# Attention and a gated MLP in one kernel: the key maxima go through DRAM, and the work around block 2's first pair of weight chunks is re-placed

## The chip, the cores and the metric

One core of a Trainium2 chip runs the kernel. The metric is the device time of one execution in microseconds (us). A core has TensorE (PE: matmuls, with their weight loads as PEld), VectorE (DVE), ScalarE (ACT), GpSimd (POOL) and SyncE (SP). In this kernel nearly every transfer between DRAM and the core's memory is issued by SP, one after the other, in the order of SP's list.

## The reference

Two softmaxes (of q over its features, of k over the sequence), two small matrix products for each head, and then a two-layer MLP over the 4608 tokens with the gate h * clip(h + 3, 0, 6) / 6:

```python
q_s = np.exp(q - np.max(q, axis=-1, keepdims=True))
q_s = q_s / (np.sum(q_s, axis=-1, keepdims=True) + 1e-09)
k_s = np.exp(k - np.max(k, axis=2, keepdims=True))          # max over the 576 positions
k_s = k_s / (np.sum(k_s, axis=2, keepdims=True) + 1e-09)
kv = np.einsum('bhsd,bhse->bhde', k_s, v)
x = np.einsum('bhsd,bhde->bhse', q_s, kv)                   # (8, 8, 576, 64), then 4608 x 512
h = x @ w_in                                                # 4608 x 2048
g = h * np.clip(h + 3.0, 0.0, 6.0) / 6.0
return g @ w_out                                            # 4608 x 512
```

q, k and v are float32, the weights are float64. Every float32 operand of a large product is split into a high and a low part, and three products (high by high, high by low, low by high) stand for one.

## The kernel before

The 4608 tokens are 9 blocks j of 512, the 2048 hidden features are 16 chunks f of 128. Blocks 0 and 1 go chunk by chunk (`gemm1`, then `gemm2`). From block 2 on (`FAST = 2`) two chunks make a pair, and `fast_pair` computes the pair's first product with 7 half-size products (Strassen's scheme in Winograd's form) instead of 8; each is 6 matmuls of 256 columns. `product(n, ...)` writes one of three PSUM tiles: z (shown as `pz`), x and y (both `ph`, two buffers). The x tile is written four times in a pair and must be emptied in between: by ACT's copies (lines 544, 555, 563), and at the end by `swish(r[:, HT:], x)`, an ACT operation (line 534) and then a DVE one (line 535). The next pair's product 1 writes the same buffer.

Between the products, `fill(n)` issues n matmuls of the second product (`po`, 512 columns) for the chunks that are pending. A usual pair has 7 x 6 half-size matmuls and 24 `po` matmuls. After each stretch `tick(j, n)` runs the steps that a table sets for that place: block j + 1's attention is spread over block j's 64 ticks, 8 to a pair. `half(j, a, b, begin)` holds the table for two of the four head pairs; its first numbers are ticks relative to `begin`. The steps that matter here: `load_k` (the transposed keys `kt`, one buffer), `k_max` (the maximum of each key feature over the sequence, `km`, one number to a partition), `k_turn` (a TensorE transpose of `km`, spread over 128 columns, against the identity: afterwards every partition holds all 128 maxima, in PSUM as `pm`), `k_sub` and `k_exp` (the keys `ke` less these maxima, then the exponential), and the q steps (`q_stat`, `q_swap`, `q_sub`, `q_exp`, `q_over`, `q_mul`, `q_turn`). `pm` takes a buffer of the pool `ps_a` (two buffers), from which `pz`, `pkv` and `px` come as well.

The weights' sums for a pair (`fast_weights`) are made in block 1 for pairs 0 to 6 and stored to DRAM. For pair 7 they are made in block 2, in six pieces that `next(pieces)` runs at ticks. Their intermediate sums s12 and s34 take the two `ob` buffers, which also hold block 1's results until their store to DRAM has landed.

What sets the order: PE keeps the program's order from block 1 on; DVE, ACT and POOL keep it from block 2 on. SP's list is laid out by the framework's scheduler, and SP waits at each transfer for what that transfer needs (data, a free buffer), with all later ones queued behind it. The ring of weights that SP fetches (`w<-wf`) holds 12 products, so that a fetch is issued when its place comes free and is needed 12 products later.

Of the kernel before, what the change touches and what calls it, by code (L numbers as in the profile page):

```python
# [10 lines left out]
F32 = mybir.dt.float32  # L11
# [3 lines left out]
ALU = mybir.AluOpType  # L15
# [3 lines left out]
P = 128  # L19
TB = 512  # L20
# [10 lines left out]
def attention_moe(  # L31
# [27 lines left out]
    nc = tc.nc  # L59

    B, NP, _, S = kT.shape
    D = q.shape[5]
    NT, DM = out.shape
    NB = NT // TB
    NFC = w.shape[0]
    NCC = DM // P
    NTT = TB // P
    NCH = S // P + 1
# [5 lines left out]
    att = ctx.enter_context(tc.tile_pool(name="att", bufs=1))  # L74
    xp = ctx.enter_context(tc.tile_pool(name="xp", bufs=2))
    moe = ctx.enter_context(tc.tile_pool(name="moe", bufs=2))
    dr = ctx.enter_context(tc.tile_pool(name="dr", bufs=1, space=bass.MemoryType.DRAM))
    ps_a = ctx.enter_context(tc.tile_pool(name="ps_a", bufs=2, space=PSUM))
# [6 lines left out]
    def ordered(ins):  # L85
        if in_order:
            tc.keep_in_program_order(ins)
# [8 lines left out]
    def flip(out, in_):  # L96
        ordered(nc.tensor.transpose(out, in_, ident))  # L97
# [23 lines left out]
    def split(hi, lo, src, engine=nc.vector):  # L121

        nc.scalar.copy(hi, src)  # L123
        engine.tensor_sub(lo, src, hi.bitcast(F32))  # L124

    def load_w(f, sides=(0, 1)):
        if f not in raws:
            raws[f] = place(f, U32, f"raw{f}")
        a, b = 2 * DM * sides[0], 2 * DM * (sides[-1] + 1)
        nc.sync.dma_start(  # L130
            raws[f][:, a:b], w[f].rearrange("p s n -> p (s n)")[:, a:b]
        )
# [39 lines left out]
    FAST = 2  # L172
# [235 lines left out]
    X11, X21, X22, T1, T2, T3, T4 = range(7)  # L408
# [46 lines left out]
    def fast_weights(pair):  # L455

        a, b = wi[2 * pair], wi[2 * pair + 1]
        kept[pair] = d = dr.tile([P, 7, 2, HT], F32, name=f"wf{pair}")
        for n, src in ((A11, a[:, :, 0:HT]), (A12, a[:, :, HT:]), (A22, b[:, :, HT:])):
            nc.sync.dma_start(d[:, n], src.bitcast(F32))  # L460
        whole = moe.tile([P, 2 * DM], F32, name="m", tag="v", bufs=3)
        for at, src in ((0, a), (TB, b)):
            nc.vector.tensor_add(
                whole[:, at : at + TB], src[:, 0].bitcast(F32), src[:, 1].bitcast(F32)
            )
            yield
        a11, a12, a21, a22 = (whole[:, n * HT : (n + 1) * HT] for n in range(4))
        hi, lo = (t.rearrange("p e n -> p (e n)") for t in (a, b))
        s12, s34 = (moe.tile([P, DM], F32, name="ob", bufs=2) for _ in range(2))
        s1, s2, s3, s4 = (t[:, n : n + HT] for t in (s12, s34) for n in (0, HT))  # L470
        nc.vector.tensor_add(s1, a21, a22)
        nc.vector.tensor_sub(s2, s1, a11)
        yield
        split(hi[:, 0:TB], lo[:, 0:TB], s12)
        yield
        nc.vector.tensor_sub(s3, a11, a21)
        nc.vector.tensor_sub(s4, a12, s2)
        yield
        split(hi[:, TB:], lo[:, TB:], s34)
        for e, t in enumerate((hi, lo)):  # L480
            nc.sync.dma_start(
                d[:, S1 : S4 + 1, e], t.bitcast(F32).rearrange("p (k n) -> p k n", k=4)
            )
# [10 lines left out]
    def fetch(count):  # L494
        for _ in range(count):
            key = next(wanted, None)
            if key is None:
                return
            j, pair, n = key
            f, h = RING[next(turn) % len(RING)]  # L500
            t = wi[f].rearrange("p a n -> p (a n)")[:, h * TB : (h + 1) * TB]
            t = t.rearrange("p (e n) -> p e n", e=2)
            nc.sync.dma_start(t.bitcast(F32), kept[pair][:, ORDER[n][0]])
            come[key] = t
# [80 lines left out]
    plan = {}  # L585
# [4 lines left out]

    def half(j, a, b, begin):

        kts, kes, vts, qts, kms, qms, swaps, qTs = ({} for _ in range(8))
        has_k = j < B
        i = a % 2
        to = factors(j)
# [6 lines left out]
        has = {}  # L603
# [17 lines left out]
                kms[hp] = att.tile([P, 1], F32, name="km", bufs=2)  # L621
                nc.vector.tensor_reduce(kms[hp], kts[hp], axis=AX.X, op=ALU.max)  # L622

        def k_turn(hp):
            if has_k:
                has["pm"] = ps_a.tile([P, TB], F32, name="pm", tag="pa")
                flip(has["pm"][:, 0:P], kms[hp].broadcast_to([P, P]))

        def k_sub(hp):
            if has_k:  # L630
                ke, pm = kes[hp], has["pm"][:, 0:P].rearrange("p (o n) -> p o n", o=1)
                nc.vector.tensor_sub(ke, ke, pm.broadcast_to([P, NCH, P]))

        def k_exp(hp):
            if has_k:
# [101 lines left out]
        def part(n, src):  # L737
            return lambda: split(to[n][:, 0, i], to[n][:, 1, i], src())

        def ts(n):  # L740
            return has["ts"][:, n * HT : (n + 1) * HT]
# [27 lines left out]
        def on(fn, *args):  # L769
            return lambda: fn(*args)  # L770
# [2 lines left out]
            (-12, on(load_k, a)),  # L773
            (-11, on(load, a)),
            (-8, on(load, b)),
            (0, on(k_max, a)),
            (1, on(load_k, b)),
            (1, on(q_stat, a, ALU.max)),
            (2, on(k_turn, a)),
            (2, on(q_swap, a)),  # L780
            (3, on(k_sub, a)),
            (4, on(k_exp, a)),
            (4, on(q_sub, a)),
            (5, on(q_exp, a)),
            (5, on(k_max, b)),
            (6, on(q_stat, a, ALU.add)),
            (7, on(q_swap, a)),
            (7, on(q_stat, b, ALU.max)),
            (8, on(q_over, a)),
            (8, on(q_swap, b)),  # L790
            (9, on(q_mul, a)),
            (10, on(q_turn, a)),
            (10, on(k_turn, b)),
            (11, on(q_hi, a)),
            (11, on(k_sub, b)),
            (12, on(q_lo, a)),
            (12, on(k_exp, b)),
            (13, on(q_sub, b)),
            (14, on(q_exp, b)),
            (15, on(q_stat, b, ALU.add)),  # L800
            (16, kv_mm),
            (16, on(q_swap, b)),
            (17, kv_out),
            (18, on(q_over, b)),
            (19, kv_parts),
            (20, on(q_mul, b)),
            (21, on(x_mm, a)),
            (21, on(q_turn, b)),
# [2 lines left out]
            (23, on(q_hi, b)),  # L811
            (24, x_t1),
            (24, on(q_lo, b)),
            (25, part(T1, lambda: ts(1))),
            (26, on(x_mm, b)),
            (27, x_both),
            (28, x_t23),
            (29, t_both),
            (30, x_t4),
            (30, part(T4, lambda: ts(0))),  # L820
        ]
        for at, fn in steps:
            n = (j - 1 - FAST) * 64 + begin + at
            n = max(n, 0)
            plan.setdefault((FAST + n // 64, n % 64), []).append(fn)

    def gemm1(j, f):
        x_hi, x_lo = x_tiles[j]
        ph = ps_h.tile([P, TB], F32, name="ph", tag="ph")
        for cc in range(NCC):  # L830
            first, last = cc == 0, cc == NCC - 1
            w_hi, w_lo = (wi[f][:, i, cc * P : (cc + 1) * P] for i in (0, 1))
            mm(ph, w_hi, x_hi[:, cc, :], first, False)
            mm(ph, w_hi, x_lo[:, cc, :], False, False)
            mm(ph, w_lo, x_hi[:, cc, :], False, last)
        g = moe.tile([P, TB], F32, name="g", bufs=2)
        nc.scalar.activation(g, ph, AF.Relu, bias=three, scale=1.0)
        nc.vector.scalar_tensor_tensor(g, g, 6.0, ph, op0=ALU.min, op1=ALU.mult)  # L838
        g_hi = moe.tile([P, TB], F32R, name="g_hi", bufs=3)
        g_lo = moe.tile([P, TB], F32R, name="g_lo", bufs=3)  # L840
        split(g_hi, g_lo, g)
        return g_hi, g_lo
# [73 lines left out]
    pend = []  # L916
# [28 lines left out]
    def fill_one():  # L945
        for got in pend.pop(0):
            run(got)

    for j in range(FAST):
        for f in range(NFC):  # L950
            if j == 0:
                if f + AHEAD < NFC:
                    load_w(f + AHEAD)
            elif not in_order:
                in_order.append(True)
                while pend:
                    fill_one()
            g = gemm1(j, f)
            if j == 0:
                if f + 2 < NFC:  # L960
                    decode(f + 2)
            elif f % 2:
                if f < 15:
                    for _ in fast_weights(f // 2):
                        pass
                if f >= 7:
                    fetch(1 if f < 15 else 12 - len(come))
            next(step, None)

            while len(pend) > 1 - j:  # L970
                fill_one()
            pend.append(work(j, [f], [g]))
    for j in range(FAST + 1, NB):
        lead = 3 if j == FAST + 1 else 0
        half(j, 0, 2, lead)
        half(j, 1, 3, 32 + min(lead, 2))
    pieces = fast_weights(NFC // 2 - 1)
    for n in range(6):
        plan.setdefault((FAST, n), []).append(lambda: next(pieces, None))
    with tc.manual_schedule(engines=ORDERED):  # L980
        for j in range(FAST, NB):
            for pair in range(NFC // 2):
# [66 lines left out]
```

## Time and profile before

| | |
|---|---|
| median of 3 runs | 879.63 us (879.42 to 879.89) |
| the profiled execution | 879.97 us, of which the profile's span is 878.2 us |
| TensorE busy | 849.6 us, 97% of the span |
| VectorE, ScalarE, GpSimd busy | 625.0 us, 453.2 us, 86.4 us |
| blocks 2 to 8 | from 237.3 us to the end |
| mean granted TensorE clock | 0.99 |

A row of the timeline gives start, duration, engine, line, operation, output <- inputs, and how many instructions it merges; in brackets stands the idle time of the engine just before and what ended it. [...] In a table by stretches, each engine has its busy time and, in brackets, the count of instructions; then come the granted clock and the DMA share.

### The profile page before, as it was taken

How to read it: one execution, taken by the hardware profiler on the slowest of the kernel's cores; microseconds unless marked ns; L12 is line 12 of the kernel's file. 1: busy time of each engine (PE TensorE's matmuls, PEld its weight loads, DVE VectorE, ACT ScalarE, POOL GpSimd, SP SyncE). 2: the span in 40 equal slices, each digit the busy share in tenths (PEclk: the TensorE clock that was granted, in tenths of full speed). 3: DMA queues.
4: the chain of work that ended last, by engine and by line, in shares of the span. 5: the costliest groups of instructions: out<-in, count | busy, mean ns of one | idle time of the engine just before them, and what ended most of it. 6: DMA issues, size and time to landing. Idle time of an engine off the chain costs nothing.

```text
span 878.2 us, 15157 instructions
## 1 busy us (share of the span) xinstructions
PE 849.6 (97%) x5380; PEld 737.0 (84%) x5380; DVE 625.0 (71%) x1271; ACT 453.2 (52%) x907; POOL 86.4 (10%) x256
## 2 busy tenths in 40 slices
PE   4899999999989999999999999999999999999998
PEld 3577777788878898988989898989898998999996
DVE  7999997777486768676767686767767676664333
ACT  7999754444344445444545454545454444444333
POOL 5000121110110101010101011010101020100000
PEclk9799999999999999999999999999999999999999
DMA  9995554538287677867686768676865675556541
GB/s 370 413 381 141 132 153 141 165 111 292 77 269 229 202 240 224 256 198 233 213 272 194 232 202 286 186 244 197 269 207 172 177 241 176 173 168 216 177 137 48
DMA packets 98203, 184.67 MB, mean 210 GB/s; under 512 B 9808, under 2 KB 24144, under 8 KB 96080
## 3 DMA queue, kind: packets, MB, share of 16 engines
q1 hardware_dynamic: 96192, 180.03, 63.4%
q0 software_dynamic: 1360, 2.62, 1.7%
q8 instruction: 43, 0.70, 0.3%
q10 hardware_dynamic: 576, 1.05, 0.3%
q14 instruction: 32, 0.26, 0.1%
HBM read 156.93 MB, written 24.12 MB: 206 GB/s over the span
## 4 chain that ended last, share of the span: by engine, by line
PE 83%; ACT 2%; DVE 2%; DMA 2%; issue 0%; SPq 0%; ACTq 0%
PE po L91 41%; PE ph L91 32%; PE pz L91 4%; PE px L91 3%; PE pkv L91 2%; DMA w<-v 1%; DMA kt<-in_kT_dram 1%; DMA out_dram<-ob 0%; ACT w L123 0%; DVE w L124 0%; ACT g L578 0%; PE pm L97 0%; ACT v L148 0%; DVE km L622 0%; DVE x_lo L124 0%
## 5 line engine op out<-in xcount | busy, mean ns | idle before, releaser
L91 PE MATMUL po<-w,w 128*128 128x512 f32 x1008 | 263.0, 395 | 0.0
L91 PEld LDWEIGHTS po<-w,w 128*128 128x128 f32 x1008 | 177.1, 189 | 28.9
L91 PE MATMUL ph<-w,w 128*128 128x256 f32 x1008 | 148.1, 283 | 3.3 <-DVE g L535 2.6
L91 PEld LDWEIGHTS ph<-w,w 128*128 128x128 f32 x1008 | 139.6, 189 | 12.9 <-DVE g L535 2.8
L91 PE MATMUL ph<-x_lo,w 128*128 128x256 f32 (+1 forms) x800 | 142.1, 303 | 0.1
L91 PE MATMUL ph<-x_hi,w 128*128 128x256 f32 (+1 forms) x592 | 138.3, 337 | 1.9 <-DVE g L838 1.2
L91 PEld LDWEIGHTS ph<-x_lo,w 128*128 128x128 f32 x800 | 112.1, 190 | 10.9 <-issue 0.4
L91 PEld LDWEIGHTS ph<-x_hi,w 128*128 128x128 f32 x592 | 96.1, 191 | 19.3 <-DVE x_lo L124 2.0
L649 POOL COPY swap<-qm 32x16 f32<-32x16 f32 x192 | 53.8, 280 | 488.7 <-DVE qm L643 482.5
L91 PE MATMUL po<-w 128*128 128x512 f32 x336 | 88.4, 395 | 0.0
L578 ACT ACTIVATE g<-second,three 128x512 f32<-128x512 f32 x56 | 40.5, 724 | 68.0 <-DVE second L576 65.7
L91 PE MATMUL po<-w,g_hi 128*128 128x512 f32 x256 | 67.9, 402 | 1.0 <-ACT g_hi L123 1.0
L91 PEld LDWEIGHTS po<-w 128*128 128x128 f32 x336 | 58.8, 189 | 10.3 <-ACT w L581 0.5
L534 ACT ACTIVATE g<-ph,three 128x256 f32<-128x256 f32 x56 | 26.6, 474 | 66.3 <-PE ph L91 66.1
L91 PEld LDWEIGHTS po<-w,g_hi 128*128 128x128 f32 x256 | 46.9, 188 | 12.1 <-ACT g_hi L123 1.1
L124 DVE TENSOR_TENSOR w<-g,w 128x512 fp32r<-128x512 f32 x56 | 38.8, 693 | 23.4 <-ACT w L123 21.6
L580 DVE SCALAR_TENSOR_TENSOR g<-g,second 128x512 f32<-128x512 f32 x56 | 38.7, 690 | 21.6 <-ACT g L578 21.5
L535 DVE SCALAR_TENSOR_TENSOR g<-g,ph 128x256 f32<-128x256 f32 x56 | 23.5, 420 | 42.7 <-ACT g L534 42.6
L582 DVE TENSOR_TENSOR w<-g,w 128x512 fp32r<-128x512 f32 x56 | 38.7, 691 | 17.3 <-ACT w L581 16.1
L564 DVE TENSOR_TENSOR second<-second,ph 128x256 f32<-128x256 f32 x56 | 23.6, 421 | 37.6 <-ACT second L563 37.5
L563 ACT COPY second<-ph 128x256 f32<-128x256 f32 x56 | 20.8, 372 | 55.8 <-PE ph L91 55.8
L91 PE MATMUL pz<-x_hi,w 128*128 128x256 f32 x336 | 49.1, 282 | 0.0
(152 smaller groups left out, 1237.5 us busy)
## 6 DMA issues: line engine op xcount, KB each, us to landing
w<-wf SPq DMA_DIRECT2D x392, 256.0 KB, 3.0
raw<-in_w_dram SPq DMA_DIRECT2D x16, 1024.0 KB, 13.4
out_dram<-ob SPq DMA_DIRECT2D x36, 256.0 KB, 3.4
vt<-in_v_dram SPq DMA_DIRECT2D x28, 325.0 KB, 5.0
wf<-w SPq DMA_DIRECT2D x16, 512.0 KB, 4.2
kt<-in_kT_dram SPq DMA_DIRECT2D x28, 288.0 KB, 3.4
ke<-in_k_dram SPq DMA_DIRECT2D x24, 320.0 KB, 4.2
qt<-in_qf_dram SPq DMA_DIRECT2D x28, 256.0 KB, 3.1
```

The source lines that it names most:

```text
L91: nc.tensor.matmul(out, lhsT, rhs, start=start, stop=stop, skip_group_check=goes_on)
L124: engine.tensor_sub(lo, src, hi.bitcast(F32))
L534: nc.scalar.activation(r, h, AF.Relu, bias=three, scale=1.0)
L535: nc.vector.scalar_tensor_tensor(r, r, 6.0, h, op0=ALU.min, op1=ALU.mult)
L563: nc.scalar.copy(second[:, HT:], x)
L564: nc.vector.tensor_add(second[:, HT:], second[:, HT:], y)
L578: nc.scalar.activation(r, second, AF.Relu, bias=three, scale=1.0)
L580: nc.vector.scalar_tensor_tensor(r, r, 6.0, second, op0=ALU.min, op1=ALU.mult)
L582: rest.append(lambda: nc.vector.tensor_sub(two[1], r, two[0].bitcast(F32)))
L649: nc.gpsimd.tensor_copy(swaps[hp][r : r + QD], qms[hp][o : o + QD])
```

## The change

Three things change.

1. From block 3's attention on, the maxima are spread without TensorE. `k_row` sends `km` (128 partitions, 4 bytes each) to a row of 512 bytes in DRAM, and `k_all` reads this row back into all 128 partitions (`kb`, in the core's memory). `k_sub` reads `kb` instead of the PSUM tile. Block 2's attention, which is written elsewhere, keeps its four transposes; 20 of the 24 go.
2. In block 2's first pair, the last chunk but one of block 1 is no longer finished ahead of the pair: its 12 `po` matmuls stay pending and are issued as fills in the pair, which then has 24. Pair 7's weight sums use a buffer of the pool tag `v` instead of the two `ob` buffers, and their six pieces run at ticks 0, 1, 3, 4, 5 and 8, ahead of the other steps there, instead of at 0 to 5 behind them.
3. In the table, `k_max` of the first head pair moves one tick later, the two `k_sub` move to ticks 9 and 12 (from 3 and 11), `q_stat` of the second head pair moves to tick 3 (from 7), other q steps follow, and the last steps of the x factors (`x_t4` and its split) move from tick 30 to 31 and 32. Block 3's first half starts 5 ticks late instead of 3.

```diff
-        s12, s34 = (moe.tile([P, DM], F32, name="ob", bufs=2) for _ in range(2))
+        if pair < NFC // 2 - 1:
+            s12, s34 = (moe.tile([P, DM], F32, name="ob", bufs=2) for _ in range(2))
+        else:
+            both = moe.tile([P, 2 * DM], F32, name="s", tag="v", bufs=3)
+            s12, s34 = both[:, 0:TB], both[:, TB:]
...
-        def k_turn(hp):
+        def k_row(hp):
             if has_k:
-                has["pm"] = ps_a.tile([P, TB], F32, name="pm", tag="pa")
-                flip(has["pm"][:, 0:P], kms[hp].broadcast_to([P, P]))
+                rows[hp] = dr.tile([1, P], F32, name=f"row{j}_{hp}")
+                nc.sync.dma_start(rows[hp].rearrange("o p -> p o"), kms[hp])
+
+        def k_all(hp):
+            if has_k:
+                kbs[hp] = att.tile([P, P], F32, name="kb", tag="kv", bufs=5)
+                nc.sync.dma_start(kbs[hp], rows[hp].broadcast_to([P, P]))
 
         def k_sub(hp):
             if has_k:
-                ke, pm = kes[hp], has["pm"][:, 0:P].rearrange("p (o n) -> p o n", o=1)
-                nc.vector.tensor_sub(ke, ke, pm.broadcast_to([P, NCH, P]))
+                over_c = kbs[hp].rearrange("p (o n) -> p o n", o=1).broadcast_to([P, NCH, P])
+                nc.vector.tensor_sub(kes[hp], kes[hp], over_c)
...
-            (3, on(k_sub, a)),
...
+            (9, on(k_sub, a)),
...
-            while len(pend) > 1 - j:
+            while len(pend) > (j == 0 or f == NFC - 1):
                 fill_one()
             pend.append(work(j, [f], [g]))
     for j in range(FAST + 1, NB):
-        lead = 3 if j == FAST + 1 else 0
+        lead = 5 if j == FAST + 1 else 0
         half(j, 0, 2, lead)
         half(j, 1, 3, 32 + min(lead, 2))
     pieces = fast_weights(NFC // 2 - 1)
-    for n in range(6):
-        plan.setdefault((FAST, n), []).append(lambda: next(pieces, None))
+    for n in (0, 1, 3, 4, 5, 8):
+        plan.setdefault((FAST, n), []).insert(0, lambda: next(pieces, None))
```

TensorE's list where block 2 begins, before. The names: `w_1068` and `w_1135` are chunks 14 and 15, `g_hi` and `g_lo` their gate outputs; the first `pz` row is product 0 of block 2's first pair.

```order
L91 MATMUL po<-w_1068,g_hi 128x512 x8
L91 MATMUL po<-w_1068,g_lo 128x512 x4
L91 MATMUL pz<-x_hi_310,w_588 128x256 x6
L91 MATMUL ph<-w_305,w_588 128x256 x6
L91 MATMUL po<-w_1135,g_hi 128x512 x2
L91 MATMUL po<-w_1135,g_lo 128x512
L91 MATMUL po<-w_1135,g_hi 128x512
L91 MATMUL ph<-x_lo_311,w_657 128x256 x12
```

The same place after:

```order
L91 MATMUL pz<-x_hi_310,w_588 128x256 x6
L91 MATMUL ph<-w_305,w_588 128x256 x6
L91 MATMUL po<-w_1068,g_hi 128x512 x4
L91 MATMUL ph<-x_lo_311,w_657 128x256 x12
L91 MATMUL po<-w_1068,g_hi 128x512 x4
L91 MATMUL po<-w_1068,g_lo 128x512 x3
L91 MATMUL ph<-w_333,w_717 128x256 x6
L91 MATMUL po<-w_1068,g_lo 128x512
```

Chunk 14's 12 matmuls moved from ahead of the pair to between its products; the pair's products moved ahead by as much.

VectorE's list late in the same pair, before. `ob<-po` is block 1's result, `ob<-m` and `ob<-m,ob` are pair 7's sums s3 and s4, `w_1135<-ob,w_1068` is the low part of their split, `g<-g,ph` empties the x tile.

```order
L870 TENSOR_SCALAR ob<-po 128x512
L643 TENSOR_REDUCE qm<-qt 128x16
L476 TENSOR_TENSOR ob<-m 128x256
L477 TENSOR_TENSOR ob<-m,ob 128x256
L124 TENSOR_TENSOR w_1135<-ob,w_1068 128x512
L535 SCALAR_TENSOR_TENSOR g<-g,ph 128x256
L632 TENSOR_TENSOR ke<-ke,pm 128x640
L124 TENSOR_TENSOR w_958<-g,w_958 128x512
```

And after (its line numbers are 4 to 11 higher):

```order
L881 TENSOR_SCALAR ob<-po 128x512
L480 TENSOR_TENSOR s<-m 128x256
L481 TENSOR_TENSOR s<-m,s 128x256
L539 SCALAR_TENSOR_TENSOR g<-g,ph 128x256
L626 TENSOR_REDUCE km<-kt 128x1
L124 TENSOR_TENSOR w_958<-g,w_958 128x512
```

The sums write `s` instead of `ob`; the split's low part and the `qm` reduction moved behind `g<-g,ph`, and the key maximum stands behind it too.

SP's list in block 3's first pair (block 4's attention), before. `kt` is the load of the second head pair's keys, and the second `kt` row that of the next half's.

```order
L608 DMA kt<-in_kT_dram 128x576
L503 DMA w_831<-wf_1614 128x512
L873 DMA out_dram<-ob 128x512
L503 DMA w_831<-wf_1614 128x512
L873 DMA out_dram<-ob 128x512
L608 DMA kt<-in_kT_dram 128x576
L873 DMA out_dram<-ob 128x512
L503 DMA w_900<-wf_1614 128x512 x2
L503 DMA w_588<-wf_1614 128x512
L873 DMA out_dram<-ob 128x512
```

And after:

```order
L612 DMA kt<-in_kT_dram 128x576
L631 DMA row_0_4504<-km 128x1
L884 DMA out_dram<-ob 128x512
L507 DMA w_831<-wf_1614 128x512
L636 DMA kb<-row_0_4504 128x128
L884 DMA out_dram<-ob 128x512
L631 DMA row_2_4568<-km 128x1
L884 DMA out_dram<-ob 128x512
L507 DMA w_900<-wf_1614 128x512
L636 DMA kb<-row_2_4568 128x128
L507 DMA w_900<-wf_1614 128x512
L884 DMA out_dram<-ob 128x512
```

Each `kb` waits in SP's list for its `row` to land, and result stores and weight fetches stand behind it; the next half's `kt` moved further back.

More of the change, by code (lines that the diff above doesn't have):

```diff
@@ L591, in half @@
     def half(j, a, b, begin):
-        kts, kes, vts, qts, kms, qms, swaps, qTs = ({} for _ in range(8))
+        kts, kes, vts, qts, kms, kbs, rows, qms, swaps, qTs = ({} for _ in range(10))
         has_k = j < B
@@ L775, in half @@
             (-8, on(load, b)),
[L776 to L780, printed above, removed]
-            (3, on(k_sub, a)),
-            (4, on(k_exp, a)),
+            (1, on(k_max, a)),
+            (2, on(load_k, b)),
+            (2, on(k_row, a)),
+            (2, on(q_stat, a, ALU.max)),
+            (3, on(k_all, a)),
+            (3, on(q_swap, a)),
+            (3, on(q_stat, b, ALU.max)),
             (4, on(q_sub, a)),
+            (4, on(q_swap, b)),
+            (5, on(k_max, b)),
             (5, on(q_exp, a)),
[L785 to L800, printed above, removed]
+            (6, on(k_row, b)),
+            (7, on(k_all, b)),
+            (9, on(k_sub, a)),
+            (10, on(k_exp, a)),
+            (10, on(q_stat, a, ALU.add)),
+            (11, on(q_swap, a)),
+            (11, on(q_sub, b)),
+            (12, on(k_sub, b)),
+            (12, on(q_exp, b)),
+            (13, on(k_exp, b)),
+            (13, on(q_over, a)),
+            (13, on(q_mul, a)),
+            (14, on(q_turn, a)),
+            (15, on(q_hi, a)),
             (16, kv_mm),
-            (16, on(q_swap, b)),
             (17, kv_out),
-            (18, on(q_over, b)),
+            (18, on(q_lo, a)),
+            (18, on(q_stat, b, ALU.add)),
             (19, kv_parts),
+            (19, on(q_swap, b)),
+            (20, on(q_over, b)),
             (20, on(q_mul, b)),
@@ L813, in half @@
             (24, on(q_lo, b)),
-            (25, part(T1, lambda: ts(1))),
+            (26, part(T1, lambda: ts(1))),
             (26, on(x_mm, b)),
@@ L818, in half @@
             (29, t_both),
-            (30, x_t4),
-            (30, part(T4, lambda: ts(0))),
+            (31, x_t4),
+            (32, part(T4, lambda: ts(0))),
         ]
```

## The prediction

> **What bounds the kernel.** I read the page first, then TensorE's waits from block 2 on, then its timeline pair by pair, and then the engine that each gap names.
>
> ```profile
> PE 849.6 (97%) x5380; PEld 737.0 (84%) x5380; DVE 625.0 (71%) x1271; ACT 453.2 (52%) x907; POOL 86.4 (10%) x256
> ...
> PE 83%; ACT 2%; DVE 2%; DMA 2%; issue 0%; SPq 0%; ACTq 0%
> ...
> PE ph L91 <- DVE g L535: 2.6, 1, 2.6
> PE pm L97 <- DVE km L622: 1.8, 2, 0.9
> PE ph L91 <- ACT second L555: 0.7, 1, 0.7
> ```
>
> TensorE is busy for 97% and is 83% of the chain that ended last. After 237 us it waits visibly four times, 5.1 us in all. So a gain can come from matmuls that go and from these few gaps; any work that another engine gains or loses counts only if TensorE has to wait for it. The pace, from the `pz` rows that open a pair:
>
> ```profile
> 805.12 0.88 PE L91 MATMUL pz<-x_hi,w 128*128 128x256 f32 x6
> 815.64 0.88 PE L91 MATMUL pz<-x_hi,w 128*128 128x256 f32 x6
> ...
> 651.48 0.88 PE L91 MATMUL pz<-x_hi,w 128*128 128x256 f32 x6
> 655.95 0.27 PE L97 MATMUL pm<-ident,km 128*128 128x128 f32 x1
> 662.13 0.88 PE L91 MATMUL pz<-x_hi,w 128*128 128x256 f32 x6
> ```
>
> A bare pair takes 815.64 - 805.12 = 10.52 us. One with a transpose takes 662.13 - 651.48 = 10.65 us: a transpose costs 0.13 us of TensorE's time, not the 0.27 us of its row. These are the pairs that are longer than that:
>
> ```profile
> 244.73 0.29 PE L97 MATMUL pm<-ident,km 128*128 128x128 f32 x1 [0.90 <-DVE km L622]
> ...
> 249.94 1.49 PE L91 MATMUL ph<-w,w 128*128 128x256 f32 x6 [2.57 <-DVE g L535]
> ...
> 285.57 0.87 PE L91 MATMUL pz<-x_hi,w 128*128 128x256 f32 x6
> 291.79 0.98 PE L91 MATMUL ph<-w,w 128*128 128x256 f32 x6 [0.69 <-ACT second L555]
> 297.21 0.87 PE L91 MATMUL pz<-x_hi,w 128*128 128x256 f32 x6
> ...
> 331.99 0.87 PE L91 MATMUL pz<-x_hi,w 128*128 128x256 f32 x6
> 337.62 0.29 PE L97 MATMUL pm<-ident,km 128*128 128x128 f32 x1 [0.87 <-DVE km L622]
> 343.82 0.88 PE L91 MATMUL pz<-x_hi,w 128*128 128x256 f32 x6
> ...
> 616.09 0.88 PE L91 MATMUL pz<-x_hi,w 128*128 128x256 f32 x6
> 627.07 0.87 PE L91 MATMUL pz<-x_hi,w 128*128 128x256 f32 x6
> ```
>
> **Block 2's first two pairs.** The stretch from the end of chunk 15's first product (234.53) to the third pair (261.49) holds chunk 14's 12 fills, two pairs with 12 and 24 fills, and two transposes. Without the transposes this is exactly the matmuls of two bare pairs, as in 697.18 to 718.22:
>
> ```profile
> 234.53:261.49 26.96, 23.49 (x135) 20.58 (x134) 19.01 (x38) 11.56 (x23) 2.86 (x12) 0.94 0.69 224
> 697.18:718.22 21.04, 21.04 (x135) 19.02 (x134) 15.18 (x33) 10.98 (x22) 3.44 (x12) 1.00 0.75 238
> ...
> 251.00:252.00 1.00, 1.00 (x5) 0.89 (x4) 0.97 (x4) 0.31 (x1) 0.00 (x0) 0.50 1.08 383
> ```
>
> So 26.96 - 21.04 = 5.92 us are lost here: 0.90 and 2.57 us of waiting, 2 x 0.13 us of transposes, and the rest mostly behind the long gap, where the granted clock is 0.50. The long gap's chain:
>
> ```profile
> 247.41 0.42 DVE L476 TENSOR_TENSOR ob<-m 128x256 f32<-128x256 f32 x1 [0.59 <-DMA out_dram<-ob]
> ...
> 249.47 0.41 DVE L535 SCALAR_TENSOR_TENSOR g<-g,ph 128x256 f32<-128x256 f32 x1
> ...
> 248.21 0.62 ACT L123 CAST w<-ob 128x512 fp32r<-128x512 f32 x1 [3.36 <-DVE ob L477]
> 248.74 0.47 ACT L534 ACTIVATE g<-ph,three 128x256 f32<-128x256 f32 x1
> ```
>
> DVE's sum s3 waits until a result store has freed `ob`; ACT's cast waits for that sum; the two operations that empty the x tile stand behind both, and TensorE waits for them. The change takes `ob` out of this, puts s3 and s4 ahead and the cast and the split's low part behind the emptying, and gives TensorE 24 fills in this pair instead of 12. I laid the new lists of DVE and ACT out by hand with the durations of the rows. The first pair comes out without a wait: x is emptied some 9.7 us after the pair's start, and the next product 1 stands at 11.3. In the second pair ACT's exponential of q (`q_exp`, at tick 5 + 5 = 10) stands ahead of the copy that frees x for product 5, waits for DVE, and TensorE waits 0.5 us. Bounds of what remains: nothing, or again the 2.57 us. I take 0.5, which is nearest to the 0.69 us that the same kind of queueing (ACT behind a DVE step of the attention) cost at 291.79. Term: 0.5 - 5.92 = -5.4 us.
>
> [...]
>
> **The other transposes.** Two of the 20 lie in that stretch. The other 18 x 0.13 = -2.3 us, straight off TensorE's list. The two long pairs: 297.21 - 285.57 = 11.64, less 10.65, is 0.99 us, where ACT's and DVE's x steps met the next half's first steps; block 3's first half starts two ticks later now, but its last steps stay in this pair, so I leave 0.2: -0.8 us. 343.82 - 331.99 = 11.83 is 1.18 us over, mostly the transpose's wait for `km`, which no transpose waits for any longer; 0.2 may remain: -1.0 us. 627.07 - 616.09 = 10.98 is 0.33 us over; its cause, a late `kt`, can return, so it counts as nothing.
>
> **What is added.** DVE's work hardly changes: `k_sub` reads `kb` instead of PSUM, 640 columns as before. What decides is when its inputs come.
>
> ```profile
> L643 DVE TENSOR_REDUCE qm<-qt 128x16 f32<-128x512 f32 x37 | 25.1, 679 | 0.0
> L632 DVE TENSOR_TENSOR ke<-ke,pm 128x640 f32<-128x640 f32 x18 | 14.4, 798 | 0.0
> ...
> 518.73 0.38 SPq L608 DMA_DIRECT2D kt<-in_kT_dram  x1
> ...
> 522.98 0.74 DVE L622 TENSOR_REDUCE km<-kt 128x1 f32<-128x576 f32 x1
> 523.64 0.41 DVE L535 SCALAR_TENSOR_TENSOR g<-g,ph 128x256 f32<-128x256 f32 x1
> ...
> 525.71 0.88 PE L91 MATMUL ph<-w,w 128*128 128x256 f32 x6
> ...
> 532.45 0.42 DVE L564 TENSOR_TENSOR second<-second,ph 128x256 f32<-128x256 f32 x1 [0.25 <-ACT second L563]
> ```
>
> This is block 5's first pair. x is emptied at 524.05 and wanted at 525.71: DVE may run 1.66 us later. Ahead of that place come one more `q_stat` (0.68) and `x_t4` with its split (0.42 each, one of them in idle time), and `k_sub` goes (0.80): 0.3 to 0.7 us later, so about 1 us of room stays. `k_max` of the second head pair stands there too, and its `kt` is asked for about 1.5 us later than the 4.4 us after the pair's start of the SP row, since the first `k_max` is a tick later.
>
> ```profile
> DMA to landing us min/median/max: 2.9/3.6/5.0
> ...
> DMA to landing us min/median/max: 2.6/3.0/6.7
> ...
> DMA to landing us min/median/max: 2.0/3.4/6.4
> ```
>
> These are `kt` after 240 us, the weight fetches `wf` after 262 us, and the result stores. With 3.6 us `kt` lands 9.5 us after the pair's start, about when `k_max` wants it; with 5.0 us TensorE waits some 0.8 us. I count half of one such wait: +0.4 us.
>
> The two transfers of `km` have no row. Each is a small one, 128 pieces of 4 or of 512 bytes. Bounds for one: 2.0 us (the quickest store) and 6.7 us (the slowest fetch); I take the medians of the same directions, 3.4 us for the write and 3.0 us for the read, since both queue behind the same bulk transfers. The second head pair is the tight one: `km` is ready about 10.2 us after its pair's start, and `k_sub` stands behind the L564 of the next pair, at 18.1 us plus 0.4. 8.3 us less two issues of 0.35 leaves 7.6 us, and 6.4 are needed. Behind `k_sub`, DVE has some 1.3 us more before the x tile is late, so TensorE sees it from 8.9 us on. Behind the waiting `kb`, SP holds up to two fetches and two stores for about 3 us: the fetches are wanted 12 products, or 18 us, later, and the stores free buffers only for the next block. The 40 new issues themselves lie in SP's gaps. Cost: nothing, as long as that cover holds.
>
> **The sum.** The profiled execution took 879.97 us (span 878.2 and 1.8 us around it). -5.4 - 2.3 - 0.8 - 1.0 + 0.4 = -9.1 gives 870.9 us. The median of the runs is 0.3 us below that execution, so I predict 870.5 us. If every wait goes, -5.92 - 2.3 - 0.99 - 1.18 - 0.33 = -10.7 gives 868.9. About 0.2% (1.8 us) is what a measurement of this kernel can tell from no change.
>
> **Rivals.**
>
> *A smaller gain.* New waits in the first pair of each of the ten halves, because `k_max` finds its `kt` late: for it speaks that the room is only about 1 us and that one load in 19 took 5.0 us; against it, the median of 3.6. Half of the ten at 0.8 us is +4, and block 2's second pair may keep 1 to 2 us more: 873 to 877 us.
>
> *Slower: `kb` comes late.* DVE, which runs in order, then stands at `k_sub` and TensorE behind it, in ten halves. It starts at 8.9 us for the two transfers and eats the whole gain at 9.8 (ten times 0.9 us). With both at the slowest rows (6.4 + 6.7 = 13.1) it is 10 x 4.2 = 42 us: 912 us; at 11 us, 891. For it: SP's order puts stores and fetches between them, in the stretch where stores took longest. Against: medians of 6.4.
> [...]
>
> *No change.* The removed waits come back one place later (DVE is the next late engine, 19.01 us busy in the 26.96). Against: the same stretch without these waits needs 21.04. About 878 to 881 us.
>
> **Chances.** Forecast, 868.8 to 872.7: 0.62. Smaller gain, up to 877.8: 0.28. No change: 0.03. Slower: 0.07. Range 868.8 to 876.2: outside it lie the last two cases and the outer part of the second. Faster 0.90, the same 0.03, slower 0.07.
>
> **What would show it.** Right: pairs of 10.52 us in blocks 2 to 6, where no `pkv` or `px` stands; 21 to 21.6 us for the first two of block 2 with 24 fills each, at a clock of 1.00; no `pm` after block 2's attention; `kb` landing before DVE stands at `k_sub`. Wrong: waits of `ke` for DMA `kb`, of `km` for DMA `kt`, and of `ph` for DVE or ACT in the first two pairs of a half; a clock under 1.00 after 237 us.

## The result, and the profile after

| | before | after |
|---|---|---|
| median | 879.63 us | 1006.69 us (1005.44 to 1009.6, 5 runs) |
| span of the profiled execution | 878.2 us | 1007.8 us |
| mean granted TensorE clock | 0.99 | 0.944 |

The ratio is 1.145, 95% interval 1.1437 to 1.1461: the change costs 127 us. The prediction was 870.5 us. Of all runs below one, of `e_four_v`, went at a granted clock of 0.656 and took 1187 us; it is left out of that kernel's median.

The page of the changed kernel: busy time, the chain that ended last (by engine, then by line), and the group of `k_sub`.

```profile
PE 885.3 (88%) x5360; PEld 760.8 (75%) x5360; DVE 625.8 (62%) x1271; ACT 452.5 (45%) x907; POOL 84.8 (8%) x256
...
PE 53%; DMA 22%; DVE 10%; ACT 5%; issue 1%; SPq 1%; ACTq 0%; POOL 0%; DVEq 0%; POOLq 0%
...
L641 DVE TENSOR_TENSOR ke<-ke,kb 128x640 f32<-128x640 f32 x20 | 16.5, 825 | 111.1 <-DMA kb<-row 111.1
```

Before, TensorE was 83% of the chain; now a fifth of it is transfers. VectorE's work is unchanged (625.0 us before, 625.8 now), but it stands 111.1 us in front of 20 subtractions that take 16.5 us. TensorE is busy 35.7 us longer than before with 20 transposes fewer: its granted clock, 0.944 at the mean against 0.99, is lower around the gaps, as in this stretch of the changed kernel (block 4's second pair):

```profile
485.90:506.20 20.30, 13.16 (x69) 10.92 (x68) 6.58 (x14) 4.67 (x9) 1.30 (x4) 0.83 0.64 58
```

A bare pair needs 10.5 us of TensorE; here it was 13.16 at a clock of 0.83, and the rest of the 20.30 us is waiting.

The waits of the changed kernel (in all, times, longest):

```profile
DVE ke L641 <- DMA kb<-row: 111.1, 19, 9.8
...
PE ph L91 <- DVE g L539: 55.8, 10, 8.9
...
PE ph L91 <- ACT second L567: 21.3, 8, 6.8
...
DVE km L626 <- DMA kt<-in_kT_dram: 20.0, 8, 7.1
```

DVE waits for `kb`; TensorE then waits for the x tile, which DVE and ACT empty late. These are the waits that the rival "`kb` comes late" named. The timeline of block 3's first three pairs shows one half; `pz` rows open the pairs, SP rows are issues:

```profile
363.96 0.42 SPq L631 DMA_DIRECT2D row<-km  x1
...
367.36 0.88 PE L91 MATMUL pz<-x_hi,w 128*128 128x256 f32 x6
...
373.64 0.32 SPq L636 DMA_DIRECT2D kb<-row  x1
...
375.58 0.38 SPq L631 DMA_DIRECT2D row<-km  x1
...
377.17 0.82 DVE L641 TENSOR_TENSOR ke<-ke,kb 128x640 f32<-128x640 f32 x1 [3.83 <-DMA kb<-row]
...
383.55 0.86 PE L91 MATMUL pz<-x_hi,w 128*128 128x256 f32 x6
...
385.28 0.32 SPq L636 DMA_DIRECT2D kb<-row  x1
...
389.86 0.82 DVE L641 TENSOR_TENSOR ke<-ke,kb 128x640 f32<-128x640 f32 x1 [9.79 <-DMA kb<-row]
...
406.19 0.87 PE L91 MATMUL pz<-x_hi,w 128*128 128x256 f32 x6
```

SP can issue the read only once the row has landed: 373.64 - 363.96 = 9.7 us, and again 385.28 - 375.58 = 9.7 us. The landings of all 20 rows, and of all 20 reads:

```profile
DMA to landing us min/median/max: 7.7/9.1/11.5
...
DMA to landing us min/median/max: 3.0/4.4/7.8
```

For the row 3.4 us had been taken, for the read 3.0. The second head pair's row is not sent before the first one's read, so a half needs 389.86 - 363.96 = 25.9 us, and the second and third pairs here take 16.19 and 22.64 us instead of 10.65 and 12.70. Against `e_pool_v` below, the other nine halves lose 12 to 16 us in these two pairs as well; blocks 7 and 8, which have no keys to prepare, are as before.

### The profile page after: what moved, and what is told of

It is laid out like the page before. It is cut to its first block, busy times and chain, and to the rows that moved or that the text cites. A ratio compares the mean times of both kernels' runs of the same rounds, so it can differ in the third digit from the quotient of the medians.

```text
span 1007.8 us, 15187 instructions
## 1 busy us (share of the span) xinstructions
PE 885.3 (88%) x5360; PEld 760.8 (75%) x5360; DVE 625.8 (62%) x1271; ACT 452.5 (45%) x907; POOL 84.8 (8%) x256
## 4 chain that ended last, share of the span: by engine, by line
PE 53%; DMA 22%; DVE 10%; ACT 5%; issue 1%; SPq 1%; ACTq 0%; POOL 0%; DVEq 0%; POOLq 0%
PE po L91 25%; PE ph L91 21%; DMA row<-km 14%; DMA kb<-row 5%; PE px L91 2%; DMA kt<-in_kT_dram 2%; PE pkv L91 2%; PE pz L91 2%; DMA w<-v 1%; ACT w L123 1%; DVE w L124 1%; DVE g L539 1%; ACT g L582 1%; DVE km L626 1%; DVE ke L641 1%
## 5 line engine op out<-in xcount | busy, mean ns | idle before, releaser
L91 PE MATMUL po<-w,w 128*128 128x512 f32 x1008 | 274.8, 409 | 5.7 <-ACT w L123 5.7
L91 PEld LDWEIGHTS po<-w,w 128*128 128x128 f32 x1008 | 186.7, 198 | 36.6 <-ACT w L123 5.9
L91 PE MATMUL ph<-w,w 128*128 128x256 f32 x1008 | 156.1, 293 | 59.2 <-DVE g L539 55.8
L91 PEld LDWEIGHTS ph<-w,w 128*128 128x128 f32 x1008 | 146.2, 198 | 71.6 <-DVE g L539 58.0
L91 PE MATMUL ph<-x_hi,w 128*128 128x256 f32 (+1 forms) x592 | 141.9, 345 | 22.7 <-ACT second L567 21.3
L91 PE MATMUL ph<-x_lo,w 128*128 128x256 f32 (+1 forms) x800 | 146.9, 308 | 9.0 <-DVE second L580 8.0
L91 PEld LDWEIGHTS ph<-x_lo,w 128*128 128x128 f32 x800 | 114.5, 194 | 23.5 <-DVE second L580 10.6
L641 DVE TENSOR_TENSOR ke<-ke,kb 128x640 f32<-128x640 f32 x20 | 16.5, 825 | 111.1 <-DMA kb<-row 111.1
L645 ACT ACTIVATE ke<-ke 128x640 f32<-128x640 f32 x20 | 14.7, 735 | 104.5 <-DVE ke L641 104.4
L123 ACT CAST w<-g 128x512 fp32r<-128x512 f32 x56 | 34.7, 620 | 45.3 <-DVE g L539 37.3
```

The costliest lines, as they stand in the source:

```text
L91: nc.tensor.matmul(out, lhsT, rhs, start=start, stop=stop, skip_group_check=goes_on)
L641: nc.vector.tensor_sub(kes[hp], kes[hp], over_c)
L645: nc.scalar.activation(kes[hp], kes[hp], AF.Exp)
```

## The experiments

**What makes the row slow: `m_quiet`, `m_more`.** Two kernels that only move data, in `m_quiet` one transfer at a time.

```diff
+row = d("row", 1, P)
+send(row.rearrange("o p -> p o"), km[:, 0:1], row[0:1, 0:1])
...
+t = d("st64", P, 16)                      # the same 4-byte pieces, 64 bytes apart
+send(t[:, 0:1], km[:, 0:1], t[0:1, 0:1])
```

> A kernel that only moves data, one transfer at a time with nothing beside it (each starts when the one before was read back), three times over: km (128 partitions x 4 bytes) into one DRAM row of 512 bytes, also with 16, 32 and 64 of its partitions; the same 4-byte pieces 64 and 512 bytes apart in DRAM; pieces of 64 and 512 bytes; 4 pieces of 128 bytes; the 4-byte pieces into the core's memory (one row, or each to its own partition); and the row read into 128 partitions. It computes nothing of the reference. Theory A (many 4-byte pieces that share one stretch of DRAM are written one after another): the row takes about 9 us here too, less in proportion for 16, 32 and 64 pieces (about 3, 4 and 5.5), 512 bytes apart about 2.5, larger pieces 2 to 3, into the core's memory about 2. Theory B (queueing behind the other traffic): everything 2 to 3 us here. Theory C (a 4-byte write to DRAM is slow wherever it goes): 9 us at every distance, 2 to 3 with larger pieces or in the core's memory. Theory D (128 pieces as such): about 9 in the core's memory and with 64- or 512-byte pieces too.

In the timeline of `m_quiet` a transfer lasts from its issue to the next `back` issue, which waits for it. In order: the row of 128 pieces, 4-byte pieces 64 bytes apart (`st`), a row in the core's memory (`srow`).

```profile
133.43 0.35 SPq L78 DMA_DIRECT2D row<-km  x1
140.67 0.24 SPq L79 DMA_DIRECT2D back<-row  x1
...
163.20 0.34 SPq L78 DMA_DIRECT2D st<-km  x1
164.77 0.22 SPq L79 DMA_DIRECT2D back<-st  x1
...
177.95 0.53 SPq L78 DMA_DIRECT2D srow<-km  x1
179.94 0.63 SPq L79 DMA_DIRECT2D back<-srow  x1
```

The row needs 7.2 us with nothing beside it, so B (queueing) falls. The same 128 pieces 64 bytes apart need 1.6 us (1.5 at 512 bytes), so C falls; in the core's memory 2.0, so D falls. A stands as far as this: the same 4-byte pieces take 7.2 us side by side in DRAM and 1.6 us apart. The DMA view of the row's 7.2 us (133.43 to 140.67, in 40 slices, busy share in tenths) shows where:

```profile
DMA  0000120000000000000000000000000000000000
...
DMA packets 144, 0.00 MB, mean 0 GB/s; under 512 B 144, under 2 KB 144, under 8 KB 144
```

All 144 packet records lie within 1.1 us of the issue; for the other 6 us nothing of the row is recorded, and what it waits for there is not shown. The count does not work as expected, though: 16, 32 and 64 pieces took 1.7, 3.3 and 6.2 us, 128 only 7.2.

> A second kernel that only moves data, in quiet and three times over; it computes nothing of the reference. 128 pieces of 4 bytes at distances of 8, 16 and 32 bytes; 128 pieces of 16 and of 32 bytes side by side; a load of 288 KB (kt) alone, behind a contiguous row, and behind a row with its pieces 64 bytes apart; and two contiguous rows, one right behind the other. If pieces that share a stretch of 64 bytes are written one after another: times fall from 7.2 us with the distance (8 bytes about 4, 16 about 3, 32 about 2), the same for larger pieces side by side. If what others see is only the row's own delay, the load behind it takes about 3 us as alone. If the queues stand still meanwhile, the load behind the contiguous row takes about 9 us, behind the spread one about 3, and the second of two rows about 14.

In `m_more`'s timeline: pieces 8 bytes (`stra`) and 16 bytes (`strb`) apart; the load of 288 KB alone (`biga`), behind a contiguous row (`six`, `bigb`), and behind a row spread to 64 bytes (`ten`, `bigc`).

```profile
76.37 0.32 SPq L78 DMA_DIRECT2D stra<-km  x1
79.16 0.24 SPq L79 DMA_DIRECT2D back<-stra  x1
81.39 0.33 SPq L78 DMA_DIRECT2D strb<-km  x1
82.85 0.23 SPq L79 DMA_DIRECT2D back<-strb  x1
...
94.08 0.33 SPq L78 DMA_DIRECT2D biga<-in_kT_dram  x1
97.10 0.59 SPq L79 DMA_DIRECT2D back<-biga  x1
...
109.99 0.41 SPq L78 DMA_DIRECT2D bigb<-in_kT_dram  x1
120.34 0.59 SPq L79 DMA_DIRECT2D back<-bigb  x1
...
122.47 0.42 SPq L78 DMA_DIRECT2D bigc<-in_kT_dram  x1
125.70 0.60 SPq L79 DMA_DIRECT2D back<-bigc  x1
```

At 8 bytes it takes 2.8 us, from 16 bytes on 1.5; the extra time is gone from 16 bytes on, where I had written 64. And others pay: a load that takes 3.0 us alone takes 10.4 behind a contiguous row, 3.2 behind the spread one. Its own packets take longer, not only its end comes late: in the DMA view they took 37.1% of the 16 engines' time over the 3.0 us alone, and with the row 63.3% over 10.8 us, an estimated 18 and 109 us when the engines are added up; the row's own packets took 1.1% of 7.2 us in `m_quiet`. Two contiguous rows sent together are through after 7.5 to 9.0 us, not 14.

**The same inside the kernel: `e_four`, `e_apart`.** `e_four` sends 4 pieces of 128 bytes:

```diff
-                nc.sync.dma_start(rows[hp].rearrange("o p -> p o"), kms[hp])
+                kr = att.tile([P, QD], F32, name="kr", bufs=2)
+                nc.vector.transpose(kr, kms[hp].broadcast_to([P, QD]))
+                nc.sync.dma_start(
+                    rows[hp].rearrange("o (b n) -> (o b) n", n=QD),
+                    kr.rearrange("(b r) n -> b r n", r=QD)[:, 0],
+                )
```

> The changed kernel, but DVE first transposes km in 32 x 32 blocks, so that the row goes to DRAM as 4 pieces of 128 bytes instead of 128 pieces of 4; the read is unchanged. Theories A, C and D (the small pieces): the row lands in 2.5 to 3.5 us, no DVE wait for kb over 1 us, pairs of blocks 3 to 6 back at 10.5 to 10.7 us, 870 to 873 us in all. Theory B (queueing): the row still takes 7 to 11 us and the time stays near 1000 us.

Measured: 881.84 us, 1.002 of the kernel before (1.0008 to 1.0036). From a row's issue to its read's issue it is now 2.4 to 5.5 us, median 2.8. So 125 of the 127 us are gone by the form of one transfer of 512 bytes. It is 9 us more than the 873 expected at most: two waits remain (`ke` for `kb`, 10.8 us in all, longest 2.5, and `km` for `kt`), which the next runs part.

`e_apart` keeps 128 pieces of 4 bytes, 64 bytes apart:

```diff
-                rows[hp] = dr.tile([1, P], F32, name=f"row{j}_{hp}")
-                nc.sync.dma_start(rows[hp].rearrange("o p -> p o"), kms[hp])
+                rows[hp] = dr.tile([P, 16], F32, name=f"row{j}_{hp}")
+                nc.sync.dma_start(rows[hp][:, 0:1], kms[hp])
...
-                nc.sync.dma_start(kbs[hp], rows[hp].broadcast_to([P, P]))
+                nc.sync.dma_start(kbs[hp][:, 0:1], rows[hp][:, 0:1])
```

> The changed kernel with the row's 128 pieces of 4 bytes put 64 bytes apart in DRAM; the read then takes 128 pieces of 4 bytes, one to a partition, so that k_sub subtracts each partition's own number and not all 128 (the maxima are not spread). Theory A (pieces that share a stretch are slow, not their size or number): the row lands in 2.5 to 3.5 us, no wait for kb over 2 us, 876 to 883 us, as with 4 pieces of 128 bytes. If 128 pieces or 4 bytes as such cost it among the other traffic: landings of 7 us and more, over 950 us.

Measured: 879.68 us, 1.0009 (0.9997 to 1.0021), landings of both kinds 1.4 to 5.2 us. Its waits:

```profile
DVE km L626 <- DMA kt<-in_kT_dram: 12.8, 8, 2.2
...
DVE ke L641 <- DMA kb<-row: 1.9, 1, 1.9
```

128 pieces of 4 bytes are harmless in the full traffic too if they lie apart. What is left is mostly `kt`. (The read is smaller here than in the changed kernel, so `e_apart` prices the write alone; `e_four` left the read as it was.)

**Is it SyncE standing still? `e_queue`.**

```diff
-                nc.sync.dma_start(kbs[hp], rows[hp].broadcast_to([P, P]))
+                nc.gpsimd.dma_start(kbs[hp], rows[hp].broadcast_to([P, P]))
...
```

> The changed kernel, but the reads of the row into 128 partitions are issued by GpSimd (steps k_all at ticks 6 and 8), so that SyncE no longer stands still until a row has landed, and the second row no longer waits behind the first read. If the landings alone cost (9.1 + 4.4 = 13.5 us against a cover of 8.9): about 4.6 us in each of ten halves, 915 to 925 us. If SyncE standing still is all of it: 871 to 880 us. If it costs nothing: 1000 us as before.

Measured: 998.23 us, 1.135 (1.1318 to 1.1375); SyncE standing still costs nearly nothing, 8.5 us of the 127; the third figure, 1000 us, is the one that came. The timeline of block 4's half (SP issues, GpSimd's reads, the first `k_sub`):

```profile
476.04 0.42 SPq L631 DMA_DIRECT2D row<-km  x1
...
479.76 0.32 SPq L631 DMA_DIRECT2D row<-km  x1
...
486.88 0.54 POOL L636 DMA_DIRECT2D kb<-row  x1 [9.19 <-ACT g L538]
495.26 0.54 POOL L636 DMA_DIRECT2D kb<-row  x1 [7.84 <-DMA row<-km]
...
499.14 0.82 DVE L641 TENSOR_TENSOR ke<-ke,kb 128x640 f32<-128x640 f32 x1 [13.52 <-DMA kb<-row]
```

The second row now goes out 3.7 us after the first, but lands 8.4 us after it, and the first read, issued at 486.88 when the first row was there, lands behind the second row, 12.2 us later. In the seven halves where the second row follows the first by 3.4 to 4.5 us, it lands 5.5 to 11.0 us after it. So a read that GpSimd issues comes late beside SP's rows too: 12.2 us, where the reads of the changed kernel took 4.4 at the median. The profiled span is 998.7 us against 1007.8.

**Can the latency be hidden? `e_early`.**

```diff
-            (1, on(k_max, a)),
-            (2, on(load_k, b)),
-            (2, on(k_row, a)),
+            (1 - early, on(k_max, a)),      # early = 10, but 0 in block 3's first half
+            (2 - early, on(load_k, b)),
+            (2 - early, on(k_row, a)),
...
```

> The changed kernel with its rows of 128 pieces, but k_max, k_row and k_all (and the second load_k) 10 ticks earlier, some 13 us, in all halves but the first of block 3. If a row only has to land in time (about 9 + 8.5 + 4.4 = 22 us from the first row to the second kb): the wait is hidden but for block 3's first half (some 15 us there), 885 to 895 us. If what costs is that all other transfers stand behind the rows' pieces in the queues (weights, kt, stores): waits for w or for kt in their place, over 910 us.

Measured: 904.96 us, 1.029 (1.026 to 1.0316), between the two. The waits for `kb` fall from 111.1 us to 10.0, both of block 3's first half, where the rows are no earlier. But `km` still waits 15.6 us for `kt` (20.0 in the changed kernel), in six places where the load went out 0.4 to 0.7 us ahead of a row and landed after 3.0 to 9.3 us, and TensorE waits 4.4 us for weights, six times, which it does neither before nor in the changed kernel. The longest wait for `kt`, behind which TensorE stood 3.4 us:

```profile
528.55 0.75 DVE L626 TENSOR_REDUCE km<-kt 128x1 f32<-128x576 f32 x1 [5.56 <-DMA kt<-in_kT_dram]
```

So earlier is far better than late, and still 25 us worse than before. About half of that is block 3's first half: one pair there (256.46 to 281.82) took 25.36 us, where 12.04 stood before. The rest lies in the other halves, with the waits for `kt` and for weights.

**The rest of the forecast: `e_turn`, `e_turn_k0`, `e_block2`.** `e_turn` has the transposes on TensorE again, one tick ahead of each `k_sub`, all else as changed:

```diff
-                nc.sync.dma_start(kbs[hp], rows[hp].broadcast_to([P, P]))
+                has["pm"] = ps_a.tile([P, TB], F32, name="pm", tag="pa")
+                flip(has["pm"][:, 0:P], kms[hp].broadcast_to([P, P]))
...
```

> The changed kernel with the maxima spread by TensorE into PSUM again, each transpose one tick ahead of its k_sub (ticks 8 and 11); block 2's start and the moved table stay as in the changed kernel. If all of the lost time is the two transfers: the forecast's other terms hold and the 18 transposes come back, 870.5 + 2.3 = 872.8 us, 871.5 to 874.5; block 2's first two pairs 21.8 us. Rival (the moved steps cost time themselves): second and third pairs of a half stay longer than 10.7 us without any transfer, 880 us or more.

Measured: 878.19 us, 0.9985 (0.9976 to 0.9993), 3.7 us above the forecast's range and below the rival's. Block 2's first two pairs took 21.78 us, as forecast, but in blocks 3 to 6 the second pairs of the halves took 10.9 to 11.9 us. To part two theories for that, the next run undoes the one tick:

```diff
-            (1, on(k_max, a)),
-            (2, on(load_k, b)),
+            (0, on(k_max, a)),
+            (1, on(load_k, b)),
```

> The run with transposes in the changed table (e_turn), but with the first k_max and the second load_k one tick earlier, at 0 and 1, as in the kernel before. Theory T (its 5 us over 872.8 are DVE waiting for the second kt, which is asked for a tick later than before): the waits of km for kt, 10.6 us in e_turn, fall under 3 us, the second pairs of a half come to 10.8 us, 872.5 to 874.5 us in all. Theory U (the q steps that moved into the second pairs crowd DVE): the second pairs stay at 10.9 to 11.8 us, 876.5 to 879 us.

Measured: 875.04 us, 0.9948 (0.9935 to 0.9962). The waits of `km` from block 2 on, in `e_turn`:

```profile
DVE km L626 <- DMA kt<-in_kT_dram: 10.6, 8, 1.7
```

and in `e_turn_k0`:

```profile
DVE km L626 <- DMA kt<-in_kT_dram: 0.4, 1, 0.4
```

Theory T holds for 3.1 of the 5.4 us: one tick for one reduction and the load behind it. The second pairs in the first half of a block stay at 11.07 to 11.09 us in blocks 3 to 6, in the other half at 10.74: a rest for theory U, and the time is 0.5 us above T's range.

`e_block2` is the kernel before with the second part of the change alone:

```diff
+            both = moe.tile([P, 2 * DM], F32, name="s", tag="v", bufs=3)
...
-            while len(pend) > 1 - j:
+            while len(pend) > (j == 0 or f == NFC - 1):
...
-    for n in range(6):
-        plan.setdefault((FAST, n), []).append(lambda: next(pieces, None))
+    for n in (0, 1, 3, 4, 5, 8):
+        plan.setdefault((FAST, n), []).insert(0, lambda: next(pieces, None))
```

> The kernel before with only the second part of the change (block 2's first pair: its 12 more fills, the weight sums' other buffer and ticks). If the forecast's term of -5.4 us stands by itself: 879.4 - 5.4 = 874.0 us, 873.3 to 874.7, with 21.8 us for block 2's first two pairs. Rival (the term only came with the moved table): a wait of over 2 us stays in the second pair, 876 to 879 us.

Measured: 876.43 us, 0.9962 (0.9949 to 0.9974): 3.0 us gained, not 5.4. The time is in the rival's range, though not by the wait that it named. By stretch (the first two pairs, the third):

```profile
235.31:257.12 21.81, 21.53 (x136) 19.14 (x135) 17.52 (x36) 10.39 (x22) 2.88 (x12) 1.00 0.81 259
257.12:270.01 12.89, 12.30 (x109) 10.74 (x108) 8.80 (x24) 6.38 (x14) 0.77 (x4) 1.00 0.82 269
```

The first two pairs are as forecast, at a clock of 1.00; the third takes 12.89 us where it took 12.04: TensorE waits 0.58 us there for ACT's first copy of x (line 548).

**Without transfers and transposes: `e_pool_v`.** After DVE's transpose in 32 x 32 blocks, GpSimd copies the blocks to the other partitions; the second `kt` gets a buffer of its own and is loaded 6 ticks earlier.

```diff
+                kb, copy = kbs[hp], nc.gpsimd.tensor_copy
+                for r in range(0, P, QD):
+                    for o in (r, r ^ QD):
+                        copy(kb[r : r + QD, o : o + QD], rows[hp][o : o + QD])
+                for r in (0, D):
+                    copy(kb[r : r + D, D - r : P - r], kb[D - r : P - r, D - r : P - r])
...
-            (2, on(load_k, b)),
+            (-4, on(load_k, b)),
```

> The changed kernel without the two transfers and without transposes on TensorE: DVE transposes km in 32 x 32 blocks (0.2 us), and GpSimd copies the blocks to the other partitions (10 copies, steps k_all at ticks 5 and 8); the second kt gets a buffer of the tag v and is loaded at tick -4. Theory T: no wait of km for kt and none of ke, pairs of 10.52 us: 868.9 to 871.0 us, the time that the forecast gave. Theory U: second pairs still over 10.9 us, 874 to 877 us. If GpSimd's 200 copies slow DVE or come late: waits of ke for GpSimd, over 872 us.

Measured: 872.1 us (871.79 to 872.42), 0.9915 (0.9902 to 0.9929): faster than both kernels and the fastest of this study, 1.1 us above Theory T's range and below Theory U's. Its timeline in block 4's second pair, and its third pair of block 2 and second pair of block 3:

```profile
428.46 0.88 PE L91 MATMUL pz<-x_hi,w 128*128 128x256 f32 x6
...
429.94 2.34 POOL L642 COPY kb<-kr 32x32 f32<-32x32 f32 x8
...
433.38 0.81 DVE L649 TENSOR_TENSOR ke<-ke,kb 128x640 f32<-128x640 f32 x1
...
438.98 0.88 PE L91 MATMUL pz<-x_hi,w 128*128 128x256 f32 x6
```

```profile
256.80:269.63 12.83, 12.26 (x109) 10.72 (x107) 8.64 (x22) 6.98 (x13) 3.62 (x12) 1.00 0.71 210
337.70:349.02 11.32, 11.02 (x69) 9.48 (x67) 8.75 (x21) 6.04 (x12) 6.84 (x22) 1.00 0.76 246
```

Ten copies take about 3 us of an idle engine and nobody waits; in blocks 4 to 6 all pairs without `pkv` or `px` take 10.52 us, as forecast. Of what lies over 870.5, these two pairs are 0.8 us each: 12.83 against 12.04 and 11.32 against 10.52. That this is just the 1.6 us is chance: block 2 also starts 0.5 us later and its first two pairs take 21.80 us where 21.54 were forecast, while the 0.4 us for a late `kt` and the 0.33 us of the long pair at 616.09 fell away.

**The forecast's own transfers: `e_four_v`, `e_four_v2`.** The row as in `e_four`, and the early `kt` as in `e_pool_v`: here the row costs about what I had taken (2.8 us to the read's issue at the median in `e_four`, 3.4 taken).

```diff
+                    kts[hp] = moe.tile([P, 2 * DM], F32, name="kt", tag="v", bufs=3)[:, 0:S]
...
-            (2, on(load_k, b)),
+            (-4, on(load_k, b)),
```

> The changed kernel with the row as 4 pieces of 128 bytes, and the second kt in a buffer of the tag v, loaded at tick -4. Here both transfers take about what the prediction gave them, and kt is early. If its other terms hold: no wait of km for kt, waits of ke for kb only where stores stand between, 870.5 to 873.5 us. If the transfers still come late (a second kb behind the first one's wait): ke waits of 10 us in all as in e_four, 876 to 879 us.

Measured: 876.75 us, 0.9971 (0.9959 to 0.9984), at the rival's end.

> The same kernel as e_four_v, for a profile at full clock: where its 4.8 us over the run without transfers (e_pool_v) lie. If in kb: waits of ke for kb of 4 to 6 us in all, in second and third pairs of a half. If in kt or elsewhere: waits of km for kt, or of TensorE for other steps, of that size.

Measured: 879.28 us in one run, beside 880.79 for the kernel before. `ke` waits 9.7 us for `kb`, seven times, and TensorE stands 2.9 us behind the longest of them. Against `e_pool_v` the third pairs of the first halves in blocks 3 to 6 took 7.0 us longer in all, 4.7 of it in block 6. Block 6's first half, SP's issues and the second `k_sub`:

```profile
611.76 0.32 SPq L644 DMA_DIRECT2D kb<-row  x1
...
613.98 0.51 SPq L636 DMA_DIRECT2D row<-kr  x1
...
618.10 0.32 SPq L644 DMA_DIRECT2D kb<-row  x1
...
623.24 0.83 DVE L649 TENSOR_TENSOR ke<-ke,kb 128x640 f32<-128x640 f32 x1 [3.92 <-DMA kb<-row]
```

The second row's data were ready at 610.8, but SP stood at the first read until 611.76 and then had stores and a fetch ahead of the row, which went out at 613.98; then 4.1 us for the row and 5.1 for the read: 12.4 us where I had 7.6 us of room.

## Why the prediction was wrong, point by point

- **The failed step: the price of the row.** "I take the medians of the same directions, 3.4 us for the write" and the upper bound of 6.7. Measured: 9.1 us at the median, 7.2 even in quiet. Rows of large transfers, however slow, did not bound a transfer of 128 neighbouring 4-byte pieces, and size alone does not price it: pieces of 4 bytes take 1.5 us when 16 bytes or more apart, 7.2 us side by side. The read was 4.4 instead of 3.0. Together 13.5 us stand where 6.4 were needed and 8.9 were covered, so "Cost: nothing" fell, and with it the sum.
- **The rival that came true, and its size.** "`kb` comes late" had 0.07 and 891 to 912 us. Its mechanism is what the waits show, but it priced 4.2 us for each half. Measured against `e_pool_v`, each half lost 13.7 us at the mean in its second and third pairs, 136.7 us in all by the two profiles. What was missing: it priced the second head pair alone, but the first one's row, read, and then the second's row and read follow each other, and a load sent behind a row landed after 10.4 us instead of 3.0 (`m_more`). That SP holds the second row behind the first read adds little: without it (`e_queue`) 8.5 us come back. "SP holds up to two fetches and two stores for about 3 us" was 7.9 and 7.3 us in block 3's first half.
- **The cover, with the row as priced.** It did not hold either: with 2.7 us for a row, `e_four_v` still lies 4.7 us above `e_pool_v`. The one profile puts that in waits for `kb`, and in block 6's first half, where it is largest, they come from the queue on SP.
- **Block 2's first two pairs:** 21.54 us forecast, 21.78 found in the changed kernel, with the wait of 0.45 us that I had left there. The clock of 0.50 after the gap went with the gap (1.00 over 235.5 to 257.3 in the changed kernel): 5.2 of the 5.9 us came back here. But 0.8 us came back in the third pair, which I had not looked at, and alone the edit brought 3.0 us instead of 5.4; part of the difference lies ahead of block 2, whose start varies from 234.4 to 235.6 us between the profiled executions (235.31 in `e_block2`, 234.53 before).
- **Transposes and long pairs:** right, by `e_pool_v`. 10.65 became 10.52; the pair of 11.64 us became 10.52 and that of 11.83 became 10.66. But the pair behind the latter went from 10.65 to 11.32, so that "0.2 may remain" was 0.8.
- **The late `kt`:** right in kind, too small. +0.4 us forecast; one tick cost 3.1 us (`e_turn` against `e_turn_k0`), since the load met DVE's wait in eight places and not in half of one.

Without the transfers and with an early `kt` the forecast of 870.5 us would have missed by 1.6 us (`e_pool_v`); with the transposes back and `kt` as late as in the change, its other terms missed by 5.4 us (`e_turn`).

## What to carry to other kernels

A row of 512 bytes took 7.2 us as 128 pieces of 4 bytes side by side and 1.5 us with the same pieces 16 bytes or more apart. So price a transfer by its pieces and by where they lie next to each other, not by its bytes or by the landings of large ones; a form that no row shows got no upper bound from the others (7.2 us in quiet against the 6.7 taken), and one quiet run of it is cheaper than the argument. Two dependent transfers in SP's list, which runs in order, cost more than their sum in `e_four_v2`: 12.4 us against landings of 4.1 and 5.1, because the second row stood in the list behind the first read, two stores and a fetch; the room was 7.6. To spread 128 numbers over the partitions, block transposes (0.2 us each on DVE) and ten copies on GpSimd, about 3 us of its idle time, were enough here.

## What the runs showed of the hardware

- 128 pieces of 4 bytes side by side in DRAM land after 7.2 us in quiet, 8 bytes apart after 2.8, from 16 bytes apart after 1.5; pieces of 16 bytes side by side also after 1.5. The same pieces into the core's memory: 2.0 us in one row, 1.8 one to a partition.
- A load behind such a row lands after 10.4 us instead of 3.0. In quiet two rows overlap (7.5 to 9.0 us for both), but in the kernel's traffic (`e_queue`) they landed 5.5 to 11.0 us apart; why is open.
- The number of pieces doesn't scale: 16, 32, 64 and 128 took 1.7, 3.3, 6.2 and 7.2 us. Why is open too.
- In the kernel before, TensorE started again at 249.94 after a gap of 2.57 us; the granted clock was 0.57 from 250 to 251, 0.50 from 251 to 252, 0.61 from 252 to 254 and 1.00 from 254 to 262.
